# Routed attention and a PReLU feed-forward: a half's attention in one clump instead of three steps

## The chip, the cores and the metric

The kernel runs on one core of one Trainium2 chip. Its time is the device time of one execution in microseconds (us). The engines are TensorE (PE, matmuls; its weight loads are listed as PEld), VectorE (DVE), ScalarE (ACT), GpSimd (POOL) and SyncE (SP, whose queue issues the DMAs). Each engine works through its own list of instructions in order and waits on semaphores for the others. Matmul operands come from SBUF, results go to PSUM, eight banks of 128 partitions x 512 FP32 values.

## The reference

There are 4 batches, 8 heads, 768 positions, head dimension 64 and 16 clusters. A query attends only to keys of its own cluster. The result, with the heads side by side, goes through a feed-forward layer (FFN) from 512 to 2048 and back to 512, with a learned slope for negative values. Everything is FP32 but the weights of the FFN, which arrive as 64-bit floats.

```python
q_assign = np.argmax(np.einsum('bhsd,hcd->bhsc', q_n, c_n), axis=-1)
k_assign = np.argmax(np.einsum('bhsd,hcd->bhsc', k_n, c_n), axis=-1)
mask = q_assign[:, :, :, None] == k_assign[:, :, None, :]
scores = np.where(mask, scale * np.matmul(q, k.transpose(0, 1, 3, 2)), -1e9)
attn = softmax(scores)                      # over the keys
x = np.matmul(attn, v)                      # (B,H,S,D) -> (B*S, H*D)
h = x @ w_in
out = (np.maximum(h, 0.0) + alpha * np.minimum(h, 0.0)) @ w_out
```

## The kernel before

**Units.** Heads are taken in pairs (`pairs`, 16 of them: 4 batches x 4). The 768 queries of a pair are two halves of 384 (`HS`), the keys six chunks of 128 (`NJ`). For a batch, first half 0 of all four pairs is done, then half 1 of all four; when the four are complete, 384 rows of the FFN's input (`xT`) are. The list `steps` holds 96 steps: batch, half, pair, and s = 0, 1, 2, each with two key chunks (`GROUP`). `UB` = 12 steps belong to one half of a batch.

**A step of attention.** `score` makes the transposed scores of two chunks for both heads (line 444: two heads in the upper and lower 64 rows of PE, side by side, into `ps_s`, two tiles of two PSUM banks) and takes their exponentials (line 460, ACT) into E tiles. `weigh` multiplies V by the E tiles of the step before (line 546, two heads in the left and right 64 columns of PE, into the one bank of `ps_v`). `mask` multiplies E by "cluster of the query equals cluster of the key" (line 469, DVE, one instruction for each chunk and head). In batch 0 the mask comes instead from an extra matmul (line 454). `add_up` sums the E tiles over the chunks (lines 482 and 487, DVE) and, after the last chunk, transposes and reduces the sum (lines 492, 495); `total` finishes the denominators with a matmul against a constant (`fold`, line 505) and `invert` takes their reciprocals and spreads them (lines 516 to 523, DVE). `normalise` multiplies the weighted values by them into `xT` (line 569, DVE). An FP32 matmul stands as two instructions in the profile, so counts of matmuls there are double.

**FFN.** `ffn_pieces` cuts the FFN of 384 rows into 28 pieces: 8 `hidden` pieces, then 6 `final` ones, then again 8 and 6. A hidden piece is four matmuls of 384 columns (line 590, into `ps_f`, two banks), then on ACT the positive part (line 597, tile gT) and the negated negative part (line 598, tile `neg`, two buffers). The slope is applied by DVE (line 582, `slopes`); it is emitted in the next hidden piece's call, and after every fourth hidden piece at once. A final piece is four matmuls of 512 columns (line 609) with gT as weights; every second one ends a PSUM bank, which ACT copies (line 615) or DVE adds to the copy (line 617), and after the last one SP sends the rows out (line 620).

**Preparation.** For a pair with first step u, `load` is called at step u-7. From batch 1 on `prep_blocks` transposes q and k on DVE at u-4, `prep_sims` makes the similarities to the centroids on PE at u-3 (line 345), and one slot later `prep_argmax` takes five DVE instructions (lines 353 to 367) to the first-ranked cluster; `prep_clusters` spreads it by PE at u-2 (line 390) and, after an ACT copy, `prep_keys` builds the keys' table; `prep_queries` transposes the queries' table at u-1, for each half. All these use the one bank of `ps_m` (`misc`).

**Order.** The program is written in the order in which each engine is to work. The main loop does, for step u: the scores of u, the weighting of u-1, the masks of u, the normalising of u-1, the sums of u, and then three slots in which FFN pieces of the half batch that is already complete, preparation and (in batch 0 and early) the conversion of FFN weights are placed. `tick` moves a slot counter on, and `later` puts a piece some slots off. FFN pieces are handed out evenly over the 12 steps; two of them (`KEEP`) are left over to the next block.

Of the kernel before, what the change touches and what calls it, by code (L numbers as in the profile page):

```python
# [21 lines left out]
def kernel(  # L22
# [36 lines left out]
    fsp = fast.enter_context(tc.tile_pool(name="fsp", bufs=4))  # L59
    aqp = fast.enter_context(tc.tile_pool(name="aqp", bufs=2))  # L60
    asg = fast.enter_context(tc.tile_pool(name="asg", bufs=1))
    raws = fast.enter_context(tc.tile_pool(name="raws", bufs=5))
    cvt = fast.enter_context(tc.tile_pool(name="cvt", bufs=3))
    epool = fast.enter_context(tc.tile_pool(name="epool", bufs=2 * GROUP))
    accp = fast.enter_context(tc.tile_pool(name="accp", bufs=2))
    rdp = fast.enter_context(tc.tile_pool(name="rdp", bufs=1))
    xpool = fast.enter_context(tc.tile_pool(name="xpool", bufs=2))
# [154 lines left out]

    CW = 512

    def convert(src, dst):
        raw = raws.tile([P, CW, 2], U32, name="raw")
        nc.sync.dma_start(out=raw.rearrange("p n w -> p (n w)"), in_=src)
        lo, hi = raw[:, :, 0], raw[:, :, 1]
        power = cvt.tile([P, CW], U32, name="power")

        def split():
            nc.vector.tensor_scalar(out=power, in0=hi, scalar1=0x7FF00000, scalar2=None,
                                    op0=ALU.bitwise_and)
            nc.vector.tensor_scalar(out=dst.bitcast(U32), in0=hi, scalar1=0x000FFFFF,
                                    scalar2=None, op0=ALU.bitwise_and)

        def scale():
            nc.scalar.activation(out=power, in_=power, func=AF.Relu,
                                 bias=low_exp[:, 0:1], scale=8.0)
            nc.scalar.activation(out=dst, in_=dst.bitcast(U32), func=AF.Identity,  # L240
                                 bias=1.0, scale=2.0 ** -20)

        def join():
            nc.vector.scalar_tensor_tensor(
                out=power, in0=hi, scalar=0x80000000, in1=power,
                op0=ALU.bitwise_and, op1=ALU.bitwise_or)
            nc.vector.scalar_tensor_tensor(  # L247
                out=dst, in0=lo, scalar=2.0 ** -52, in1=dst,
                op0=ALU.mult, op1=ALU.add)
            nc.gpsimd.tensor_tensor(out=dst, in0=dst, in1=power.bitcast(FP32),  # L250
                                    op=ALU.mult)
        return [split, scale, join]
# [177 lines left out]
             for hp in range(NCH) for s in range(SB)]  # L430
    NS = len(steps)
    UB = NCH * SB
    Es, accs, pos, rds, xTs = {}, {}, {}, {}, {}

    def score(u):
        n, half, s = steps[u]
        qkT = qkTs[n]
        chunks = range(s * GROUP, (s + 1) * GROUP)
        pss = [ps_s.tile([P, 2, 512], FP32, name="sps") for c in chunks]
        early_mask = n < NCH  # L440
        for c, ps in zip(chunks, pss):
            for h in range(2):
                r = h * D
                nc.tensor.matmul(  # L444
                    out=ps[:, h, 0:HS],
                    lhsT=qkT[r:r + D, S + c * P:S + (c + 1) * P],
                    rhs=qkT[r:r + D, half * HS:(half + 1) * HS], start=True,
                    stop=not early_mask)
        if early_mask:
            for c, ps in zip(chunks, pss):  # L450
                g, i = divmod(NJ + c, GT)
                r = slice(g * Q, (g + 1) * Q)
                for h in range(2):
                    nc.tensor.matmul(  # L454
                        out=ps[:, h, 0:HS], lhsT=members[n][r, h, i * P:(i + 1) * P],
                        rhs=aqs[n, half][r, 0, :], start=False, stop=True)
        Es[u] = []
        for ps in pss:
            E = epool.tile([P, 2, HS], FP32, name="E")
            nc.scalar.activation(out=E, in_=ps[:, :, 0:HS], func=AF.Exp, scale=SCALE)  # L460
            Es[u].append(E)

    def mask(u):
        n, half, s = steps[u]
        if n < NCH:
            return
        for c, E in zip(range(s * GROUP, (s + 1) * GROUP), Es[u]):
            for h in range(2):
                nc.vector.scalar_tensor_tensor(  # L469
                    out=E[:, h, :], in0=aqs[n, half][:, h, :],  # L470
                    scalar=keys[n][:, NJ + c, h:h + 1],
                    in1=E[:, h, :], op0=ALU.is_equal, op1=ALU.mult)

    def add_up(u):

        n, half, s = steps[u]
        if u < UB:
            return
        E = Es[u]
        if s == 0:  # L480
            acc = accp.tile([P, 2, HS], FP32, name="acc")
            nc.vector.tensor_tensor(out=acc, in0=E[0], in1=E[1], op=ALU.add)
            accs[n, half] = acc
            E = E[2:]
        acc = accs[n, half]
        for e in E:
            nc.vector.tensor_tensor(out=acc, in0=acc, in1=e, op=ALU.add)  # L487
        if s == SB - 1:


            accT = accp.tile([P, 2 * NX, Q], FP32, name="acc")
            nc.vector.transpose(out=accT.rearrange("p x i -> p (x i)"),  # L492
                                in_=acc.rearrange("p h q -> p (h q)"))
            part = rdp.tile([P, 2 * NX], FP32, name="part")
            nc.vector.tensor_reduce(out=part, in_=accT, axis=AX.X, op=ALU.add)  # L495
            parts[n, half] = part

    parts, totals = {}, {}

    def total(u):  # L500

        n, half, s = steps[u]
        if s == SB - 1 and u >= UB:
            ps = misc()
            nc.tensor.matmul(out=ps[:, 0:2 * NX], lhsT=fold, rhs=parts.pop((n, half)),  # L505
                             start=True, stop=True)
            totals[n, half] = ps

    def invert(u):

        n, half, s = steps[u]
        if (n, half) not in totals:
            return
        ps = totals.pop((n, half))
# [10 lines left out]
                in_=inv[r, h * NX:(h + 1) * NX, None].broadcast_to((D, NX, Q)))  # L525
        rds[n, half] = rd

    def weigh(u):


        n, half, s = steps[u]
        E = Es.pop(u)
        if s == 0:
            pos[n, half] = ps_v.tile([P, 512], FP32, name="vps")
        po = pos[n, half]
        if u < UB:
            for i, e in enumerate(E):
                for h in range(2):
                    r = h * D
                    nc.tensor.matmul(out=first_den[r:r + D, 0:HS], lhsT=ones,  # L540
                                     rhs=e[:, h, :], start=(s == 0 and i == 0),
                                     stop=(s == SB - 1 and i == GROUP - 1))
        for c, e in zip(range(s * GROUP, (s + 1) * GROUP), E):
            for h in range(2):
                r = h * D
                nc.tensor.matmul(out=po[r:r + D, 0:HS], lhsT=vts[n][:, h, c, :],  # L546
                                 rhs=e[:, h, :], start=(c == 0), stop=(c == NJ - 1))
        if s == SB - 1 and u < UB:


            denT = asg.tile([P, NX, Q], FP32, name="simT")
# [8 lines left out]
            nc.vector.transpose(out=rd, in_=inv[:, 0:NX, None].broadcast_to((P, NX, Q)))  # L560
            rds[n, half] = rd

    def normalise(u):
        n, half, s = steps[u]
        b, hp = pairs[n]
        if s == SB - 1:
            if (b, half) not in xTs:
                xTs[b, half] = xpool.tile([P, NCH, HS], FP32, name="xT")
            nc.vector.tensor_tensor(out=xTs[b, half][:, hp, :],
                                    in0=pos.pop((n, half))[:, 0:HS],  # L570
                                    in1=rds.pop((n, half)), op=ALU.mult)


    def ffn_pieces(b, half):
        xT = xTs[b, half]
# [27 lines left out]
        def final(i, f0, on, off):  # L603
            convert_up_to((f0 // FQ + 1) * (NCH + FQ))
            if on:
                pss[i] = ps_f.tile([P, 512], FP32, name="fps")
            ps = pss[i]
            for f in range(f0, f0 + FQ):
                nc.tensor.matmul(out=ps[:, 0:DM], lhsT=gs[f][:, i * P:(i + 1) * P],  # L609
# [25 lines left out]
    for u, (n, half, s) in enumerate(steps):  # L635
        start_of.setdefault((n, half), u)

    SLOTS, FIRST = 5, 2
    AHEAD = 4
    prep_at, load_at = {}, {}  # L640
    for (n, half), u in start_of.items():
        def at(step, slot, piece):
# [14 lines left out]

    KEEP = 2
    ffn = deque()
    for u in range(-AHEAD, NS + 1):  # L660
        for n in load_at.get(u, []):
            if n > 1:
                load(n)
        tick()
        if 0 <= u < NS:
            score(u)
        tick()
        if u > 0:
            invert(u - 1)
            weigh(u - 1)  # L670
        if 0 <= u < NS:
            mask(u)
        if u > 0:
            normalise(u - 1)
        if 0 <= u < NS:
            add_up(u)
        if u > 0 and u % UB == 0:
            early.clear()
            n, half, _ = steps[u - 1]
            ffn.extend(ffn_pieces(pairs[n][0], half))  # L680
            whole = len(ffn) - KEEP
        if u == NS:
            break
        take = (max(len(ffn) - KEEP - whole * (UB - 1 - u % UB) // UB, 0) if ffn else 0)
        converting = 0 if u < 0 else 1 + (u % 4 == 3) if u < UB else 1 + u % 2
        for i in range(SLOTS - FIRST):
            tick()
            for _ in range(take * (i + 1) // 3 - take * i // 3):
                ffn.popleft()()
            if (u, i) == (1 - AHEAD, 0):  # L690
                cT, alpha_neg = prepare_constants()
            for piece in prep_at.pop((u, FIRST + i), []):
                piece()
            if i < converting:
                convert_next()
        if 0 <= u < NS:
            total(u)
    while due:
        tick()
    good = const.tile([P, 2], FP32, name="good")  # L700
# [169 lines left out]
```

## Time and profile before

| What | Value |
|---|---|
| time, median of 3 runs | 1048.01 us (1046.67 to 1048.5) |
| the profiled execution | 1049.33 us, of which the span of instructions 1047.5 us |
| mean granted TensorE clock | 0.993 |
| PE, DVE, ACT, POOL busy | 98%, 64%, 33%, 5% of the span |
| DMA | 42.72 MB, mean 41 GB/s |

The page gives the busy time of each engine, the chain of work that ended last, and groups of instructions by line. The trace behind it can be asked for the order of time in a stretch (start, length, engine, line, operation, number of instructions run together, and in brackets how long the engine had been idle and what ended that), for the chain step by step (start, length, what), and for busy time and granted clock in chosen windows. Names before `<-` are what is written, names behind it what is read. A busy PE is not PE at its peak: matmuls overlap, and the distance between the starts of two of them is what counts.

### The profile page before, as it was taken

How to read it: one execution, taken by the hardware profiler on the slowest of the kernel's cores; microseconds unless marked ns; L12 is line 12 of the kernel's file. 1: busy time of each engine (PE TensorE's matmuls, PEld its weight loads, DVE VectorE, ACT ScalarE, POOL GpSimd, SP SyncE). 2: the span in 40 equal slices, each digit the busy share in tenths (PEclk: the TensorE clock that was granted, in tenths of full speed). 3: DMA queues.
4: the chain of work that ended last, by engine and by line, in shares of the span. 5: the costliest groups of instructions: out<-in, count | busy, mean ns of one | idle time of the engine just before them, and what ended most of it. 6: DMA issues, size and time to landing. Idle time of an engine off the chain costs nothing.

```text
span 1047.5 us, 10241 instructions
## 1 busy us (share of the span) xinstructions
PE 1027.5 (98%) x3827; PEld 483.5 (46%) x3827; DVE 675.6 (64%) x1155; ACT 345.6 (33%) x628; POOL 55.8 (5%) x71
## 2 busy tenths in 40 slices
PE   8999999799999999999999999999999999999997
PEld 4444444344454444445444444544445454544553
DVE  4896879758676564868766574876777575562111
ACT  5664443433242323314323132422323132220220
POOL 1332312200000000000000000000000000000000
PEclk9999999899999999999999999999999999999999
DMA  9542663130000230042000230033000000000000
GB/s 217 172 136 81 132 121 76 30 76 1 0 1 21 41 45 16 1 80 42 1 1 11 51 46 16 1 65 56 1 1 0 21 11 1 0 11 20 1 1 33
DMA packets 120936, 42.72 MB, mean 41 GB/s; under 512 B 113696, under 2 KB 113712, under 8 KB 120880
## 3 DMA queue, kind: packets, MB, share of 16 engines
q1 hardware_dynamic: 120704, 41.95, 18.7%
q8 instruction: 32, 0.52, 0.2%
q14 instruction: 24, 0.20, 0.1%
q10 hardware_dynamic: 176, 0.04, 0.0%
HBM read 35.69 MB, written 6.29 MB: 40 GB/s over the span
## 4 chain that ended last, share of the span: by engine, by line
PE 93%; DVE 3%; ACT 1%; DMA 1%; issue 1%; SPq 1%; POOL 0%; DVEq 0%; POOLq 0%; ACTq 0%
PE fps L609 32%; PE fps L590 32%; PE sps L444 13%; PE vps L546 12%; PE sps L454 1%; PE mps L345 1%; PE fps L540 1%; DMA raw<-in_moe_w_in_dram 1%; SPq L114 1%; ACT E L460 0%; DVE gT L582 0%; DMA qk<-in_k_dram 0%; PE mps L505 0%; ACT qk L320 0%; DVE acc L487 0%
## 5 line engine op out<-in xcount | busy, mean ns | idle before, releaser
L609 PE MATMUL fps<-w_out_sb,gT 128*128 128x512 f32 x768 | 347.0, 604 | 6.2 <-POOL w_out_sb L250 6.0
L590 PE MATMUL fps<-xT,w_in_sb 128*128 128x384 f32 x1024 | 345.6, 491 | 0.0
L590 PEld LDWEIGHTS fps<-xT,w_in_sb 128*128 128x128 f32 x1024 | 190.6, 190 | 151.0 <-ACT E L460 18.5
L469 DVE SCALAR_TENSOR_TENSOR E<-aq,key,E 128x384 f32<-128x384 bf16 x288 | 158.9, 613 | 142.5 <-ACT E L460 141.6
L609 PEld LDWEIGHTS fps<-w_out_sb,gT 128*128 128x128 f32 x768 | 142.5, 191 | 194.2 <-issue 176.8
L460 ACT ACTIVATE E<-sps 128x768 f32<-128x768 f32 x192 | 145.4, 808 | 153.8 <-PE sps L444 64.1
L597 ACT ACTIVATE gT<-fps 128x384 f32<-128x384 f32 x128 | 62.7, 490 | 339.2 <-PE fps L590 339.2
L444 PE MATMUL sps<-qkT 64*128 64x384 f32 x768 | 151.2, 512 | 0.0
L546 PE MATMUL vps<-E,vt 128*64 128x384 f32 x768 | 145.0, 499 | 0.0
L582 DVE SCALAR_TENSOR_TENSOR gT<-neg,alpha_neg,gT 128x384 f32<-128x384 f32 x128 | 82.7, 663 | 83.8 <-ACT neg L598 83.7
L487 DVE TENSOR_TENSOR acc<-acc,E 128x768 f32<-128x768 f32 x112 | 107.0, 955 | 19.4 <-ACT E L460 17.0
L444 PEld LDWEIGHTS sps<-qkT 64*128 64x128 f32 x768 | 66.6, 187 | 65.9 <-issue 34.4
L546 PEld LDWEIGHTS vps<-E,vt 128*64 128x64 f32 x768 | 47.8, 136 | 82.3 <-issue 78.6
L617 DVE TENSOR_TENSOR y<-y,fps 128x512 f32<-128x512 f32 x30 | 20.5, 683 | 80.9 <-PE fps L609 80.9
L615 ACT COPY y<-fps 128x512 f32<-128x512 f32 x24 | 14.0, 585 | 158.3 <-PE fps L609 158.3
L598 ACT ACTIVATE neg<-fps 128x384 f32<-128x384 f32 x128 | 62.2, 486 | 5.1 <-DVE gT L582 4.6
L523 DVE STREAM_TRANSPOSE rd<-inv 64x384 f32<-64x384 f32 x56 | 32.1, 573 | 0.4
L250 POOL TENSOR_TENSOR w_in_sb<-w_in_sb,power 128x512 f32<-128x512 f32 x16 | 26.4, 1654 | 85.7 <-DVE w_in_sb L247 85.7
L250 POOL TENSOR_TENSOR w_out_sb<-w_out_sb,power 128x512 f32<-128x512 f32 x16 | 24.8, 1550 | 64.6 <-DVE w_out_sb L247 64.6
L492 DVE STREAM_TRANSPOSE acc<-acc 128x768 f32<-128x768 f32 x28 | 27.4, 978 | 1.0
L495 DVE TENSOR_REDUCE part<-acc 128x24 f32<-128x768 f32 x28 | 26.7, 953 | 1.0
L320 ACT ACTIVATE qk<-qk 128x768 f32<-128x768 f32 x32 | 26.7, 845 | 0.0
(90 smaller groups left out, 434.8 us busy)
## 6 DMA issues: line engine op xcount, KB each, us to landing
raw<-in_moe_w_in_dram SPq DMA_DIRECT2D x16, 512.0 KB, 4.2
raw<-in_moe_w_out_dram SPq DMA_DIRECT2D x16, 512.0 KB, 3.6
vt<-in_v_dram SPq DMA_DIRECT2D x16, 384.0 KB, 4.6
out_dram<-y SPq DMA_DIRECT2D x24, 256.0 KB, 2.1
qk<-in_q_dram SPq DMA_DIRECT2D x48, 96.0 KB, 3.4
qk<-in_k_dram SPq DMA_DIRECT2D x48, 96.0 KB, 3.7
qk<-in_q_dram SPq DMA_DIRECT2D x8, 192.0 KB, 4.9
qk<-in_k_dram SPq DMA_DIRECT2D x8, 192.0 KB, 4.6
```

What stands on the lines that cost most here:

```text
L250: nc.gpsimd.tensor_tensor(out=dst, in0=dst, in1=power.bitcast(FP32), op=ALU.mult)
L444: nc.tensor.matmul(out=ps[:, h, 0:HS], lhsT=qkT[r:r + D, S + c * P:S + (c + 1) * P], rhs=qkT[r:r + D, half * HS:(half + 1) * HS], start=Tr ...
L460: nc.scalar.activation(out=E, in_=ps[:, :, 0:HS], func=AF.Exp, scale=SCALE)
L469: nc.vector.scalar_tensor_tensor(out=E[:, h, :], in0=aqs[n, half][:, h, :], scalar=keys[n][:, NJ + c, h:h + 1], in1=E[:, h, :], op0=ALU.is ...
L487: nc.vector.tensor_tensor(out=acc, in0=acc, in1=e, op=ALU.add)
L523: nc.vector.transpose(out=rd[r, :], in_=inv[r, h * NX:(h + 1) * NX, None].broadcast_to((D, NX, Q)))
L546: nc.tensor.matmul(out=po[r:r + D, 0:HS], lhsT=vts[n][:, h, c, :], rhs=e[:, h, :], start=(c == 0), stop=(c == NJ - 1))
L582: nc.vector.scalar_tensor_tensor(out=gs[f], in0=neg, scalar=alpha_neg[:, f:f + 1], in1=gs[f], op0=ALU.mult, op1=ALU.add)
L590: nc.tensor.matmul(out=ps[:, 0:HS], lhsT=w_in_sb[:, c, f * P:(f + 1) * P], rhs=xT[:, c, :], start=(c == 0), stop=(c == NCH - 1))
L597: nc.scalar.activation(out=gs[f], in_=ps[:, 0:HS], func=AF.Relu)
L598: nc.scalar.activation(out=neg, in_=ps[:, 0:HS], func=AF.Relu, scale=-1.0)
L609: nc.tensor.matmul(out=ps[:, 0:DM], lhsT=gs[f][:, i * P:(i + 1) * P], rhs=w_out_sb[:, f, :], start=on and f == f0, stop=off and f == f0 + ...
```

## The change

Batch 0 keeps its loop. From step `TOGETHER` = 24 on, the attention of a half stands together once every three steps: scores of chunks 0 to 2, weighting of all six chunks of the half that came ahead, masks and sums of the three, then scores, masks and sums of chunks 3 to 5. The rest of the three steps holds FFN pieces, twelve slots for each half. Since `ps_s` has room for two chunks only, chunk 2 of the first three and chunk 3 of the second three (`alone`) go to the two banks of `ps_f`, with one exponential for each head. E tiles are no longer a rotating pool but nine fixed tiles: four of their own and, once the FFN weights are converted (`more_room`), the five raw tiles of the conversion. `total` comes at the first slot of the third step and `invert` at its second, so ahead of the next clump. No FFN piece is kept over to the next block except one at the last, and a final piece that has begun a bank is followed by the one that ends it before the next clump. The steps and slots of loads and preparation are as before (those of slots 2 and 3 in a clump's step now stand behind the whole clump).

```diff
-    raws = fast.enter_context(tc.tile_pool(name="raws", bufs=5))
+    raws = fast.enter_context(tc.tile_pool(name="raws", bufs=1))
-    epool = fast.enter_context(tc.tile_pool(name="epool", bufs=2 * GROUP))
+    epool = fast.enter_context(tc.tile_pool(name="epool", bufs=1))
...
+    raw_tiles = [raws.tile([P, CW, 2], U32, name=f"raw{i}") for i in range(5)]
...
+    waiting = []
+    e_tiles = [epool.tile([P, 2, HS], FP32, name=f"E{i}") for i in range(2 * GROUP)]
+
+    def more_room():
+        for raw in raw_tiles:
+            e_tiles.insert(0, raw.rearrange("p n w -> p (n w)").bitcast(FP32)[
+                :, 0:2 * HS].rearrange("p (h q) -> p h q", h=2))
+
+    def score(n, half, chunks, alone=None):
...
+        pss = [[ps_f.tile([P, 512], FP32, name="fps") for h in range(2)] if c == alone else
+               ps_s.tile([P, 2, 512], FP32, name="sps") for c in chunks]
...
+        for c, ps in zip(chunks, pss):
+            E = e_tiles[0]
+            e_tiles.append(e_tiles.pop(0))
+            if c == alone:
+                for h in range(2):
+                    nc.scalar.activation(out=E[:, h, :], in_=ps[h][:, 0:HS], func=AF.Exp,
+                                         scale=SCALE)
+            else:
+                nc.scalar.activation(out=E, in_=ps[:, :, 0:HS], func=AF.Exp, scale=SCALE)
+            waiting.append((n, half, c, E))
...
+    for u in range(TOGETHER, NS + 1):
+        for n in load_at.get(u, []):
+            load(n)
+        if u < NS:
+            n, half, s = steps[u]
+        if s == 0 or u == NS:
+            prior = steps[u - 1][:2]
+            assert not unfinished[0]
+            tick()
+            if u < NS:
+                score(n, half, range(0, NJ // 2), alone=NJ // 2 - 1)
+            tick()
+            invert(*prior)
+            weigh(GROUP if u == TOGETHER else NJ)
+            if u < NS:
+                mask(NJ // 2)
+            normalise(*prior)
+            if u % UB == 0:
+                feed_block(u)
+                whole = len(ffn) - (NS - u <= UB)
+            if u == NS:
+                break
+            add_up(NJ // 2)
+            tick()
+            score(n, half, range(NJ // 2, NJ), alone=NJ // 2)
+            mask(NJ // 2)
+            add_up(NJ // 2)
+            slots = range(3, SLOTS)
+        else:
+            slots = range(SLOTS)
+        for i in slots:
+            tick()
+            if s == 0:
+                prepare(u, FIRST + i - 3)
+            if (s, i) == (SB - 1, 0):
+                total(n, half)
+            at_slot = (u % UB) // SB * FREE + (s * SLOTS + i - 3)
+            left = UB // SB * FREE - 1 - at_slot
+            pieces = len(ffn) - (NS - u <= UB) - whole * left // (UB // SB * FREE)
+            feed(max(pieces, 0))
+            if (s, i) == (SB - 1, SLOTS - 1) and unfinished[0]:
+                feed(1)
+            if s > 0:
+                prepare(u, i)
+            if (s, i) == (SB - 1, 1):
+                invert(n, half)
```

## The prediction

> **What bounds the kernel now.** I read the page's busy times and the chain of work first, then the chain step by step, then the order of time in one half of batch 2, then the granted clock around TensorE's three long gaps.
>
> ```profile
> PE 1027.5 (98%) x3827; PEld 483.5 (46%) x3827; DVE 675.6 (64%) x1155; ACT 345.6 (33%) x628; POOL 55.8 (5%) x71
> PE 93%; DVE 3%; ACT 1%; DMA 1%; issue 1%; SPq 1%; POOL 0%; DVEq 0%; POOLq 0%; ACTq 0%
> ```
>
> TensorE (PE) is never without work, so only what lies between matmuls can be won. The chain shows it:
>
> ```profile
> 806.30 1.49 PE sps L444 x8
> 807.79 1.44 PE vps L546 x8
> 809.23 7.06 PE fps L609 x16
> 816.29 1.49 PE sps L444 x8
> ...
> 826.29 0.14 PE mps L505 x2
> ...
> 950.43 8.76 PE fps L609 x16
> 959.19 20.64 PE fps L590 x64
> 979.83 20.60 PE fps L609 x48
> ```
>
> The last block, without attention, gives the pace: 20.64/64 = 0.3225 us for a 384-column matmul, 20.60/48 = 0.429 for a 512-column one. Scores and weightings run two heads at once, so 8 are four slots, 1.29. In a step scores take 1.49 (0.20 too much), weighting 1.44 (0.15), 16 final matmuls 7.06 against 6.87 (0.20): **0.55 us a step is lost at changes of kind**. The fold matmul adds 0.14.
>
> The order of time shows VectorE (DVE), which works its queue in order:
>
> ```profile
> 509.43 1.56 PE L444 MATMUL sps<-qkT 64*128 64x384 f32 x8
> 510.40 1.51 ACT L460 ACTIVATE E<-sps 128x768 f32<-128x768 f32 x2 [0.27 <-PE sps L444]
> 511.24 2.21 DVE L469 SCALAR_TENSOR_TENSOR E<-aq,key,E 128x384 f32<-128x384 bf16 x4 [5.56 <-ACT E L460]
> 513.36 1.94 DVE L487 TENSOR_TENSOR acc<-acc,E 128x768 f32<-128x768 f32 x2
> 515.34 0.98 DVE L492 STREAM_TRANSPOSE acc<-acc 128x768 f32<-128x768 f32 x1
> 516.35 0.95 DVE L495 TENSOR_REDUCE part<-acc 128x24 f32<-128x768 f32 x1
> 517.22 0.57 DVE L422 STREAM_TRANSPOSE aq<-every 128x384 bf16<-128x384 bf16 x1
> ```
>
> Masks follow each other by 0.53, adds by 0.98, transpose and reduction by 1.01 and 0.87. Exp starts 0.97 after scores, masks 1.81 after. The argmax that follows the centroid matmuls (L345) has five DVE instructions, 527.05 to 529.78.
>
> The clock, window by window (half-rate spans lasted 3.41 and 10.24 us, one and three times the same stretch, so I cut time in its steps; columns: stretch, length, PE busy and so on; PEclk is third from last):
>
> ```profile
> 43.14:46.55 3.41, 2.07 (x16) 1.06 (x12) 3.38 (x7) 3.41 (x7) 1.71 (x1) 1.00 0.25 36
> 46.55:49.96 3.41, 3.10 (x18) 1.60 (x20) 3.35 (x6) 1.76 (x4) 1.78 (x2) 1.00 0.75 269
> 947.67:951.08 3.41, 1.60 (x10) 0.67 (x7) 2.51 (x10) 0.00 (x0) 0.00 (x0) 1.00 0.20 77
> 951.08:954.50 3.42, 3.42 (x5) 1.33 (x5) 0.00 (x0) 0.00 (x0) 0.00 (x0) 0.50 0.00 0
> ```
>
> A stretch with 1.34 of 3.41 us idle left the clock at 1.00; one with 1.81 idle was followed by 3.42 us at half clock, where 16 final matmuls took 8.76 instead of 7.06: **1.7 us for one such stretch**.
>
> **The change part by part.** Batches 1 to 3 have 24 halves of one head pair, each three steps before, one clump after. T is time since a clump's first score.
>
> *Changes of kind.* Before, per half: 3 x 0.55 + 0.14 = 1.79. After: scores 0.20, weighting 0.15, scores again, feed-forward (FFN) 0.20, fold. Weighting-to-scores and scores-to-FFN do not occur in this trace; the second scores cost between 0.10 and 0.25 by the rows above, I take 0.20, the scores' own row. The fold moves in among FFN matmuls: two 24-column matmuls whose weight loads (190 ns) nothing covers; between 0.20 and 0.40, I take 0.33, from the 0.14 plus what FFN-to-scores costs anyway. After: 1.08. Gain 0.71 x 24 = 17.0. The centroid matmuls (11 times) now stand behind the scores rather than amid FFN, one change less, 0.20 each: -2.2. The cluster matmuls (L390, 11 times) move from behind the weighting into FFN: about +0.1 each, +1.1. **Sum -18.1**, by the bounds -24 to -15.
>
> *No cost.* PE, DVE and DMA issue the same instructions; only the two lone chunks of a half have their exp in two (0.387 + 0.49 against 0.81), with ACT 33% busy. Loads are issued at the same steps, three steps (some 30 us) ahead of their use against 5 us to land, and SP's queue holds only these and the outputs. Both ps_f banks are free at the clump: the last FFN piece's two evictions end at T=0.98, chunk 2's scores start at 1.40. Exp of chunks 0 to 2 ends at 3.26, the second scores need it at 6.15. Nine E tiles suffice for six waiting chunks and three new.
>
> *The DVE burst.* This is the cost. PE: scores of three chunks 6 x 0.3225 + 0.20 = 2.13; weighting of six, 12 x 0.3225 + 0.15 = 4.02, ends 6.15; scores 2.13, so **FFN starts at 8.28** (before it started 2.93 after the scores). DVE: six masks from 1.81 to 5.0; normalise (0.47) waits for weighting, 6.27 to 6.74; two adds (0.98 + 0.88) to 8.60; six masks to 11.78; three adds to 14.74; transpose to 15.76; reduction to **16.63**. Behind it in the queue stand the slopes (L582, pitch 0.53, done after 0.61) of hidden pieces and, in 11 halves, the argmax: 0.61 + 0.59 + 0.59 + 0.39 to its last instruction, 0.55 more to its result. A hidden piece takes 8 x 0.3225 = 2.58, a final piece 8 x 0.429 = 3.43, FFN's first 0.10 more. Seven pieces go into each clump, so clumps 0, 2, 4, 6 of a batch begin with hidden pieces, and 1, 3, 5, 7 with the last of eight hidden, the slope of the seventh still owing. Centroid matmuls (0.78) stand ahead of FFN in clumps 0, 1, 2 and (not in the last batch) 7; the cluster matmuls, which need the argmax, come only three pieces later, where before they came a step later.
>
> - Clumps 4, 6: nothing late. The third hidden's neg tile comes free at 17.3, its bank at 17.8, the fifth hidden wants it at 18.7.
> - Clumps 0, 2: FFN from 9.07, three hidden end at 8.28 + 0.78 + 0.10 + 7.74 = 16.91. The argmax is there at 16.63 + 2.18 + 0.55 + 0.06 (release) = 19.43. **PE waits 2.5**. Five such clumps (clump 0 of batch 1 is covered by two final pieces held back): 12.6.
> - Clumps 3, 5 (and 7 of batch 3): hidden to 10.97, final to 14.40, two weights of the next final to 16.12; the third needs the seventh slope, 16.63 + 0.61 + 0.06, and its weight load 0.19: 17.50. PE waits 1.38, seven times: 9.7.
> - Clumps 1, 7: 0.78 later at the same place, wait 0.60; then clusters at 19.22 against the argmax behind two slopes, 17.69 + 2.18 + 0.55 + 0.06 = 20.48, wait 1.27. Four times 1.87: 7.5. Clump 1 of batch 1, with eight pieces behind it: hidden, hidden, final end at 17.76, argmax behind one slope at 20.0: 2.2.
>
> **Sum +32.0**; each 0.1 us on the burst's end is worth 1.7. From both sides: the burst cannot start before its first exp, and 0.4 us either way is what I allow for releases and pitches, +-7.
>
> *Clock.* Idle of 2.2 to 2.5 us, six times: where it falls in one 3.41-us stretch, or over 1.6 of it does, half clock follows. With stretches placed at random that is about five in six (threshold between the 1.34 and the 1.81 seen): 5 x 1.7 = **+8.5**, between 0 and two stretches each, 20. Waits of 1.4 us I leave at full clock, the row of 1.34 being nearest. The trace itself has 203.6 to 213.8 at half clock, untouched by the change.
>
> The Trainium skill's page "TensorE: Matmul & The Clock Gate", section "HAM oscillation — how this bites in real kernels", has a rule against idle gaps over about 3.4 us; read strictly, none of these waits would cost clock and the sum would be 8.5 lower. The row of 947.67 disagrees: there a gap of 1.81 us sufficed, so I go by the row.
>
> *End.* The inversion now precedes the last weighting, so the flag matmul waits for normalise and four small instructions only: 1.2 instead of 1.8 us, which by the rows leaves the clock up: -0.6 - 1.7 = **-2.3**.
>
> Sum: -18.1 + 32.0 + 8.5 - 2.3 = +20.1. The profiled execution took 1049.33 (span 1047.5 and 1.83 around it): 1069.4. The median, 1048.01, lies 1.3 below that execution, so I say 1068.
>
> **Rivals.**
> 1. *The clock stays up* at all waits. For: the 1.34 row. Against: the 1.81 row. 1059.6.
> 2. *The clock falls further*: also at the waits of 1.4 and 1.9 us (eleven, about half of them), or for two stretches where a wait straddles them; the three stretches from 203.6, one of them 85% busy, speak for it. 10 us more, 1078.
> 3. *Faster: the burst is covered.* If DVE reaches the slopes and the argmax 0.85 us sooner than 16.63, the waits shrink to 18 and almost no clock falls, and gain and loss balance; 2 us sooner leaves some 3 us of waits, and the time is near 1031. For: DVE is only 64% busy, and 1.3 us of the burst is its wait for weighting. Against: its pitches are in every step of this trace.
> 4. *The change does not do what it says*: the two unseen changes of kind cost as much as three steps did. Then 17.0 is lost and it is 1085. Every change seen costs 0.15 to 0.20, against it.
>
> **How the numbers follow.** Forecast (1060 to 1077) 0.45; rival 1 (1050 to 1060) 0.20; rivals 2 and 4 (over 1077) 0.16; rival 3 (under 1046) 0.15; balance by chance 0.04. 0.2% (2.1 us) is about what this kernel's measurement can tell from no change. The range, 1047 to 1085, leaves out the faster case and the far end; the forecast's own range is 1060 to 1077. Faster 0.15, same 0.04, slower 0.81.
>
> **What would show it.** Right: PE idle before the cluster matmuls, ended by the argmax's last reduction, some 2.5 us; PE idle before final matmuls, ended by the slopes, 1.4 us, in the later half of each batch; short stretches at half clock after the former; changes of kind down to some 0.75 us a half; the gap before the flag matmul near 1.2. Wrong: PE as closed as before in batches 1 to 3, or DVE through its burst well before T=16.

## The result and the profile after

| | before | after |
|---|---|---|
| median of the runs | 1047.95 us (1046.67 to 1048.5, 4 runs) | 1062.31 us (1059.04 to 1064.19, 4 runs) |
| profiled execution | 1049.33 | 1059.04 |
| PE, DVE, ACT busy | 98%, 64%, 33% | 95%, 64%, 33% |

The changed kernel is slower: its time is 1.0135 of the time before, 95% interval 1.0109 to 1.0162. 1068 was forecast. The page, engines and chain:

```profile
PE 1008.8 (95%) x3827; PEld 488.5 (46%) x3827; DVE 679.3 (64%) x1155; ACT 346.4 (33%) x676; POOL 55.9 (5%) x71
PE 71%; DVE 24%; issue 1%; ACT 1%; DMA 1%; SPq 0%; POOL 0%; DVEq 0%; POOLq 0%; ACTq 0%
```

TensorE is busy 18.7 us less for the same matmuls (fewer changes of kind, and 6.83 us at half clock instead of 13.65), and yet the span grew: DVE, with the same work as before, holds 24% of the chain instead of 3%. Which waits these are, the view of PE's waits says (in all, times, longest):

```profile
PE mps L393 <- DVE first L370: 18.5, 10, 2.3
PE fps L631 <- DVE gT L603: 8.2, 12, 1.0
PE fps L611 <- DVE y L639: 2.8, 2, 2.4
PE mps L796 <- DVE good L793: 1.2, 1, 1.2
```

Before, the same view of 300 to 930 us lists no wait of PE at all. L393 are the cluster matmuls, L370 the last reduction of the argmax; L603 are the slopes. One clump (clump 2 of batch 1, T = 0 at 280.81) in order of time, PE and DVE:

```profile
280.81 1.56 PE L461 MATMUL sps<-qkT 64*128 64x384 f32 x8
...
282.62 2.20 DVE L494 SCALAR_TENSOR_TENSOR raw<-aq,key,raw 128x384 f32<-128x384 bf16 x4 [11.25 <-ACT raw L482]
...
287.08 0.56 DVE L588 TENSOR_TENSOR xT<-vps,rd 128x384 f32<-128x384 f32 x1 [1.21 <-PE vps L567]
287.56 0.95 DVE L505 TENSOR_TENSOR acc<-raw,raw 128x768 f32<-128x768 f32 x1
...
289.41 3.26 DVE L494 SCALAR_TENSOR_TENSOR E<-aq,key,E 128x384 f32<-128x384 bf16 x6
289.88 8.01 PE L611 MATMUL fps<-xT,w_in_sb 128*128 128x384 f32 x24
292.59 2.93 DVE L510 TENSOR_TENSOR acc<-acc,E 128x768 f32<-128x768 f32 x3
...
296.57 0.95 DVE L518 TENSOR_REDUCE part<-acc 128x24 f32<-128x768 f32 x1
297.44 0.57 DVE L356 STREAM_TRANSPOSE simT<-mps 128x384 f32<-128x384 f32 x1
...
299.62 0.55 DVE L370 TENSOR_REDUCE first<-top 128x24 bf16<-128x384 bf16 x1
300.23 0.26 PE L393 MATMUL mps<-first,spread 128*128 128x24 bf16 x4 [2.34 <-DVE first L370]
```

DVE's burst runs from 282.62 (T = 1.81) to the argmax's first instruction at 297.44 (T = 16.63, as worked out in the prediction). PE has done its three hidden pieces at 297.89 and stands 2.34 us until the argmax is there. In the clock's windows (columns as in the prediction), this wait and the one before the flag matmul:

```profile
296.40:299.81 3.41, 1.49 (x5) 0.57 (x3) 3.24 (x7) 0.49 (x1) 0.00 (x0) 1.00 0.00 0
299.81:303.22 3.41, 2.99 (x15) 1.93 (x15) 2.46 (x6) 0.63 (x3) 0.00 (x0) 1.00 0.02 5
...
968.82:972.23 3.41, 3.12 (x11) 1.90 (x12) 0.36 (x2) 0.12 (x1) 0.00 (x0) 1.00 0.00 0
```

Here 1.92 us of a stretch were idle and the clock stayed; no half-rate stretch shows in this execution between 211 us and the end of the matmuls. The three other runs were slower by 3 to 5 us, at mean clocks of 0.992, 0.989 and 0.992 against 0.995; they left no trace, so where their clock fell is not known.

### The profile page after: what moved, and what is told of

Read it like the earlier page. It is cut to its first block, busy times and chain, and to the rows that moved or that the text cites. A ratio compares the mean times of both kernels' runs of the same rounds, so it can differ in the third digit from the quotient of the medians.

```text
span 1057.3 us, 10220 instructions
## 1 busy us (share of the span) xinstructions
PE 1008.8 (95%) x3827; PEld 488.5 (46%) x3827; DVE 679.3 (64%) x1155; ACT 346.4 (33%) x676; POOL 55.9 (5%) x71
## 3 DMA queue, kind: packets, MB, share of 16 engines
q1 hardware_dynamic: 120704, 41.95, 18.5%
## 4 chain that ended last, share of the span: by engine, by line
PE 71%; DVE 24%; issue 1%; ACT 1%; DMA 1%; SPq 0%; POOL 0%; DVEq 0%; POOLq 0%; ACTq 0%
PE fps L631 24%; PE fps L611 24%; PE vps L567 11%; PE sps L461 7%; DVE acc L510 7%; DVE raw L494 3%; DVE E L494 2%; PE fps L461 2%; DVE acc L515 2%; DVE part L518 2%; DVE acc L505 1%; DVE gT L603 1%; PE sps L471 1%; PE fps L562 1%; DVE xT L588 1%
## 5 line engine op out<-in xcount | busy, mean ns | idle before, releaser
L603 DVE SCALAR_TENSOR_TENSOR gT<-neg,alpha_neg,gT 128x384 f32<-128x384 f32 x128 | 83.1, 666 | 97.9 <-ACT neg L619 97.5
L494 DVE SCALAR_TENSOR_TENSOR raw<-aq,key,raw 128x384 f32<-128x384 bf16 x160 | 87.3, 611 | 44.3 <-ACT raw L482 44.3
L461 PE MATMUL sps<-qkT 64*128 64x384 f32 x576 | 110.5, 502 | 0.0
L482 ACT ACTIVATE E<-sps 128x768 f32<-128x768 f32 x88 | 67.2, 813 | 82.2 <-PE sps L471 44.9
L494 DVE SCALAR_TENSOR_TENSOR E<-aq,key,E 128x384 f32<-128x384 bf16 x128 | 70.3, 611 | 20.5 <-ACT E L482 20.5
L567 PE MATMUL vps<-E,vt 128*64 128x384 f32 x448 | 81.4, 491 | 0.0
L639 DVE TENSOR_TENSOR y<-y,fps 128x512 f32<-128x512 f32 x30 | 20.5, 684 | 91.9 <-PE fps L631 91.9
L510 DVE TENSOR_TENSOR acc<-acc,E 128x768 f32<-128x768 f32 x64 | 61.2, 957 | 19.1 <-ACT E L482 16.9
L482 ACT ACTIVATE raw<-sps 128x768 f32<-128x768 f32 x56 | 42.9, 814 | 70.1 <-PE sps L461 70.1
L567 PE MATMUL vps<-raw,vt 128*64 128x384 f32 x320 | 56.5, 491 | 0.0
L510 DVE TENSOR_TENSOR acc<-acc,raw 128x768 f32<-128x768 f32 x48 | 45.8, 955 | 1.1
L461 PE MATMUL fps<-qkT 64*128 64x384 f32 x192 | 41.4, 508 | 0.0
```

Source lines behind the costliest of these rows:

```text
L461: nc.tensor.matmul(out=bank(ps, h), lhsT=qkT[r:r + D, S + c * P:S + (c + 1) * P], rhs=qkT[r:r + D, half * HS:(half + 1) * HS], start=True, ...
L494: nc.vector.scalar_tensor_tensor(out=E[:, h, :], in0=aqs[n, half][:, h, :], scalar=keys[n][:, NJ + c, h:h + 1], in1=E[:, h, :], op0=ALU.is ...
L603: nc.vector.scalar_tensor_tensor(out=gs[f], in0=neg, scalar=alpha_neg[:, f:f + 1], in1=gs[f], op0=ALU.mult, op1=ALU.add)
```

## The experiments

The theory: the gain at changes of kind is there, but a half's masks and sums, now in one piece of DVE's queue, make the argmax and the slopes late, and PE, which works in order, waits; long waits now and then cost clock. The rivals: PE is held by something else (banks, ACT), or the clump itself costs PE time. Ratios are to the kernel before on the same chip, whose medians there lay between 1045.72 and 1048.3.

### The suspected cause taken away: no masks in clumps

```diff
-            if n < NCH:
+            if n < NCH or m == NJ // 2:
                 continue
```

> The masks of the clumps are left out (twelve VectorE instructions for each half, so queries of batches 1 to 3 attend to all keys). It takes away the suspected cause: the burst ends some 3.2 us sooner (not 6.4, since the second sums then wait for the exponentials). Theory: all waits but the one of clump 0 of batch 1 go, some 30 us, and what is left is the gain from fewer changes of kind: 1028 to 1031, profile and median alike. Rival (changes of kind gain nothing, or clumps cost TensorE time by themselves): over 1040.

Measured: **1024.3** (1024.13 to 1024.74), 0.978 of before (0.976 to 0.980). The page's chain and, in PE's waits, all that is longer than 0.2 us and lies behind batch 0:

```profile
PE 95%; DVE 3%; ACT 1%; issue 1%; POOL 0%; DVEq 0%; POOLq 0%
```

```profile
PE mps L796 <- DVE good L793: 1.2, 1, 1.2
```

Of the waits behind batch 0 only the one at the end is left (L796, before the flag matmul); that of clump 0 of batch 1 is gone too. Between the profiled executions, 1059.04 and 1024.74, lie 34.3 us: the price of the waits (PE's view lists 29.5 us of idle for them; what makes the rest was not taken apart). From before's 1049.33 to 1024.74 are 24.6. How much of it is changes of kind, sixteen halves of a head pair tell, in which neither execution is at half clock: from the first scores of half 1 of batch 1 to those of half 1 of batch 3 the kernel before takes 490.87 us (335.49 to 826.36), this run 477.09 (334.70 to 811.79). That is 0.86 a half, 20.7 in 24. The end has about 2.3; the remaining 1.6 lie in batch 0, where the half-rate stretch falls on other work. The clump costs PE nothing by itself.

### One mover moved: the cluster matmuls two slots later

```diff
-                at(u - 2, FIRST, lambda n=n: prep_clusters(n))
+                at(u - 2, FIRST + 2 if u - 2 >= TOGETHER else FIRST,
+                   lambda n=n: prep_clusters(n))
```

> From the first clumps on, the cluster matmuls (L390 before, L393 after) are placed two slots later; nothing else is changed. Theory (the VectorE burst makes the argmax late, and TensorE, working in order, stands at the cluster matmuls): the 18.5 us of idle before them go. What is behind the argmax in VectorE's queue, the slopes, now holds TensorE in its place: about 1.0 us in each of the five clumps 0 and 2 at the fifth hidden piece's bank, 1.2 us in clump 1 of batch 1. So some 12.5 us off the profiled 1059: about 1047 in the profile, and a median no more than 2 us above it, since no wait is left that could pull the clock down. Rival (TensorE is held by its banks or by ScalarE, and the argmax is only the last to come): the idle moves to another line in the same size, 1059 to 1062. Rival (changes of kind became dearer): no change of time.

Measured: **1055.72** (1055.44 to 1056.91), a ratio of 1.0082 (1.0062 to 1.0102). The wait before L393 is gone, but only 3 us came of it in the profiled execution (1055.99). PE's waits, and the place in order of time:

```profile
PE mps L527 <- ACT every L397: 9.5, 11, 1.6
PE fps L631 <- DVE gT L603: 9.0, 13, 1.0
...
PE fps L611 <- ACT neg L619: 3.2, 4, 0.8
```

```profile
301.12 0.25 PE L393 MATMUL mps<-first,spread 128*128 128x24 bf16 x4
301.55 0.49 ACT L619 ACTIVATE neg<-fps 128x384 f32<-128x384 f32 x1 [2.32 <-DVE gT L603]
301.94 0.48 ACT L618 ACTIVATE gT<-fps 128x384 f32<-128x384 f32 x1
302.31 0.50 ACT L619 ACTIVATE neg<-fps 128x384 f32<-128x384 f32 x1
302.68 0.26 ACT L397 CAST every<-mps 128x96 bf16<-128x96 f32 x1
302.99 0.40 PE L527 MATMUL mps<-part,fold 128*128 128x24 f32 x2 [1.62 <-ACT every L397]
```

The waits at the hidden pieces' bank came as expected (four of 0.8). What I had not seen: two slots later the cluster matmuls stand directly ahead of the fold, and both use the one bank of `ps_m`. ACT's copy out of it stands behind three evictions that are themselves late because of the slopes. So I expected too much, by the size of a wait that took the place of the one removed.

### The same with the fold and the inversion two slots later

```diff
-            if (s, i) == (SB - 1, 0):
+            if (s, i) == (SB - 1, 2):
                 total(n, half)
...
-            if (s, i) == (SB - 1, 1):
+            if (s, i) == (SB - 1, 3):
                 invert(n, half)
```

> As the run with the cluster matmuls two slots later, and the fold two slots and the inversion two slots later, so that a feed-forward piece stands between cluster matmuls and fold. In the run without this TensorE waited 9.5 us at the fold for the cluster matmuls' bank, which ScalarE had yet to copy. Theory: that wait goes, 1055.7 - 9.5, so 1045 to 1047; left are the slopes' waits, some 12 us with the fifth hidden piece's. Rival (the fold waits for something else than the bank): 1053 to 1056.

Measured: **1046.37** (1045.29 to 1047.91), 1.0002 of before (0.9991 to 1.0013): 9.4 less than without the second step, the wait at the fold is gone, and it was the bank.

### The slope of the last hidden piece ahead of a clump emitted at once

```diff
-            if f % FQ == FQ - 1:
+            if f % FQ == FQ - 1 or f % (2 * FQ) == 2 * FQ - 2:
                 slopes()
```

> The slope of the hidden piece that stands last before a clump is emitted in that piece's own call, so ahead of the burst instead of behind it. Theory: the waits of final matmuls for gT shrink. In the seven clumps without centroid matmuls only the eighth slope is left behind the burst, 0.5 us instead of 1.4 each, 6 us; in the four with them the argmax moves up by one slope, 0.5 each, 2 us. So 8 us off: 1051 in the profile, a median near 1054; the waits of the cluster matmuls in clumps 0 and 2 stay at 2.3 us. Rival (the final matmuls wait for PSUM or the copies): 1059 to 1062, the waits as they were.

Measured: **1055.08** (1054.86 to 1056.43), a ratio of 1.0078 (1.0058 to 1.0098). The waits for gT went from 8.2 to 1.0 us; those of the cluster matmuls stayed (19.0). The profiled execution, 1054.94, shows three half-rate stretches after batch 0, two of them in these windows, each behind a wait at the cluster matmuls:

```profile
258.45:261.86 3.41, 0.86 (x4) 0.05 (x3) 3.27 (x8) 0.49 (x1) 0.00 (x0) 1.00 0.00 0
261.86:265.28 3.42, 3.42 (x8) 1.56 (x9) 0.93 (x3) 0.24 (x1) 0.00 (x0) 0.50 0.02 5
480.31:483.73 3.42, 1.07 (x7) 0.39 (x6) 3.28 (x8) 0.49 (x2) 0.00 (x0) 1.00 0.00 0
483.73:487.15 3.42, 3.42 (x7) 1.89 (x6) 1.11 (x2) 0.62 (x2) 0.00 (x0) 0.50 0.00 0
```

Three times 1.7 are 5.1: without them it would stand at 1049.8, a little under the 1051 expected.

### The gaps filled, to part the clock from the waiting

```diff
         ps = misc()
+        for _ in range((3 if n % NCH % 2 else 1) if n > NCH else 0):
+            nc.tensor.matmul(out=ps[:, 0:HS], lhsT=ident, rhs=qkTs[n][:, 0:HS],
+                             start=True, stop=True)
         for g in range(NG):
```

> Ahead of the cluster matmuls TensorE gets matmuls whose result is thrown away, three of 384 columns (1.94 us) in clumps 0 and 2, one (0.65 us) in 1 and 7, into the bank that the cluster matmuls then write. They stand where TensorE waits anyway, so the time without clock effects stays at 1059 within 1 us, while no idle gap is over 1.3 us. Theory (the runs' spread of 1059 to 1064 and their clocks of 0.995 to 0.989 come from gaps of 2.3 us that fall into one window of the clock or not): every run at 1059 to 1060, clock 0.994 to 0.995. Rival (the spread is of another origin): median 1062 and the same spread.

Measured: **1060.64**, four runs within 1060.54 to 1060.65 and one at 1062.19, clocks 0.994 to 0.996. The waits before the cluster matmuls are down to 3.5 us in all, the waits for gT unchanged at 8.2, and no half-rate stretch lies behind 212 us. The runs of the changed kernel spread over 5.2 us, and their clock falls as their time grows; with the gaps filled four of five lie within 0.1. That fits the theory but does not prove it: there are few runs, the run with the slope emitted early keeps gaps of 2.3 us and spread over 1.6 only, and the kernel before, without any of these waits, spread over 4.5 us on the same chip.

The profiled 1060.65 lies 1.6 over the changed kernel's 1059.04. The fill costs this where PE did not wait at the cluster matmuls, in clump 0 of batch 1:

```profile
231.84 2.10 PE L393 MATMUL mps<-qkT,ident 128*128 128x384 f32 x6
```

From the second scores of clump 0 to the first of clump 1 pass 30.08 us (214.52 to 244.60) instead of 28.51 (214.67 to 243.18). So the expectation that it stands only where TensorE waits anyway was wrong in this one clump. Where PE did wait, the fill cost nothing: the sixteen halves take 499.64 us, in the changed kernel 499.72. The longer half-rate stretch of this execution in batch 0 (10.24 us against 6.83) is not the reason: behind it the two kernels are level.

### The burst made longer

```diff
             parts[n, half] = part
+            spent = rdp.tile([P, 2 * NX], FP32, name="spent")
+            nc.vector.tensor_reduce(out=spent, in_=accT, axis=AX.X, op=ALU.add)
```

> The changed kernel with the last reduction of each burst done twice, the second time into a tile that nobody reads: 0.98 us more VectorE work at the end of each burst. Theory: seventeen waits grow by 0.98 each, and two sorts of clump that had 0.9 us to spare now just wait: 17 us, so 1076 in the profile if the clock stays; six waits of 3.3 us fill a window of the clock, so that half clock follows most of them, up to 10 us more: 1076 to 1088, clock 0.985 to 0.99. Rival (TensorE is not held by the burst's end): under 1066.

Measured: **1091.23** (1089.73 to 1094.63), clocks 0.976 to 0.981, a little over the range expected. PE's waits, and two pairs of windows:

```profile
PE mps L393 <- DVE first L370: 23.7, 10, 3.2
PE fps L633 <- DVE gT L605: 17.6, 12, 1.9
```

```profile
489.69:493.10 3.41, 0.71 (x3) 0.09 (x1) 3.27 (x7) 0.49 (x1) 0.00 (x0) 1.00 0.00 0
493.10:496.52 3.42, 2.92 (x9) 1.71 (x10) 2.12 (x4) 0.62 (x2) 0.00 (x0) 0.50 0.00 0
...
329.27:332.68 3.41, 1.54 (x5) 0.47 (x4) 3.38 (x5) 0.00 (x0) 0.00 (x0) 1.00 0.00 0
332.68:336.10 3.42, 3.42 (x5) 1.34 (x5) 0.28 (x2) 0.00 (x0) 0.00 (x0) 0.50 0.00 0
```

Seventeen waits grew by 0.86 to 0.87 each, the distance between two reductions that don't depend on each other rather than 0.98, 14.6 us in all. The other half of the 31 us between the profiled executions is clock: nine windows, 30.7 us, at half rate behind 214 us. At 1.7 each they are worth 15.3, more than expected, since the waits of 1.87 at the final matmuls now trigger it as well (the second pair).

### Two DVE steps exchanged

In every clump of the changed kernel behind which PE waits, but the very first, the chain goes through the weighting, here in clump 2 of batch 1:

```profile
283.01 4.04 PE vps L567 x24
287.06 0.02 issue
287.08 0.56 DVE xT L588
287.64 0.88 DVE acc L505
```

So there DVE's 1.21 us of waiting before normalise is not slack. The sums of the first three chunks need only the masks; they can go ahead of it.

```diff
-            normalise(*prior)
+            if u < NS:
+                add_up(NJ // 2)
+            normalise(*prior)
...
-            add_up(NJ // 2)
             tick()
             score(n, half, range(NJ // 2, NJ), alone=NJ // 2)
```

> The changed kernel with two VectorE steps of a clump exchanged: the sums of the first three chunks come before the normalising of the half ahead, which has to wait for TensorE's weighting. No instruction is added or left out. Theory: VectorE no longer stands 1.2 us for the weighting in mid burst; its second masks are then held by the exponentials, so the burst ends some 0.9 us sooner, and with it each of the eighteen waits: 16 us less of them, 1042 to 1044 in the profile and the median, since no gap of over 1.9 us is left to pull the clock down. Rival (that wait of VectorE is slack; what is behind it is held by ScalarE): 1057 to 1062.

Measured: **1043.15** (1042.72 to 1043.18), 0.9957 of before (0.9943 to 0.9971), and 16 us less than the profiled execution of the changed kernel. In order of time, DVE in the same clump, whose first score starts at 279.68:

```profile
284.66 0.95 DVE L505 TENSOR_TENSOR acc<-raw,raw 128x768 f32<-128x768 f32 x1
285.65 0.96 DVE L510 TENSOR_TENSOR acc<-acc,E 128x768 f32<-128x768 f32 x1
286.53 0.55 DVE L588 TENSOR_TENSOR xT<-vps,rd 128x384 f32<-128x384 f32 x1
287.30 3.29 DVE L494 SCALAR_TENSOR_TENSOR E<-aq,key,E 128x384 f32<-128x384 bf16 x6 [0.23 <-ACT E L479]
...
295.36 0.57 DVE L356 STREAM_TRANSPOSE simT<-mps 128x384 f32<-128x384 f32 x1
```

The burst ends at T = 15.68 instead of 16.63. The waits of the cluster matmuls fell from 18.5 to 11.0, those for gT from 8.2 to 0.2.

### Everything moved behind the burst

Eight hidden or six final pieces follow a clump, so no slope is owing when one begins; the argmax comes one slot later, behind the first slope; cluster matmuls and fold are moved so that a piece lies between them.

```diff
-        later(1, lambda: prep_argmax(n, ps))
+        later(2 if n > NCH else 1, lambda: prep_argmax(n, ps))
...
-                at(u - 2, FIRST, lambda n=n: prep_clusters(n))
+                at(u - 2, FIRST + 1 + u // SB % 2 if u - 2 >= TOGETHER else FIRST,
+                   lambda n=n: prep_clusters(n))
...
-            at_slot = (u % UB) // SB * FREE + (s * SLOTS + i - 3)
-            left = UB // SB * FREE - 1 - at_slot
-            pieces = len(ffn) - (NS - u <= UB) - whole * left // (UB // SB * FREE)
-            feed(max(pieces, 0))
+            slot = s * SLOTS + i - 3
+            if slot == 0:
+                share = len(ffn) - (20 if u % UB < 6 else 6) if (u // SB) % 2 == 0 else 6
+            feed(-(-share * (slot + 1) // FREE) + (share * slot // -FREE))
```

Besides, `total` and `invert` stand one slot later each.

> All that the burst held up is moved behind it, and the clump itself is left as it is: a clump is followed by eight hidden or six final pieces instead of seven of either (no slope is owing when a clump begins), the argmax is emitted one slot later (behind the first slope), the cluster matmuls one or two slots later, and the fold one slot later, so that a piece stands between the cluster matmuls and it and the bank they share is free. Theory: all waits but the one of clump 0 of batch 1 (2 to 3 us) and some 0.4 us in clumps 0 and 2 go; 1024 as without masks, plus 3 to 5: 1027 to 1030, clock 0.994, faster than before by 1.8%. Rival (a clump's VectorE work only fits when masks are left out; what is moved finds a new wait): 1040 or more.

Measured: **1026.92** (1026.76 to 1027.21), 0.9812 of before (0.9791 to 0.9833). This version, with its masks, beats both kernels, and by the most. PE's waits behind batch 0:

```profile
PE fps L611 <- DVE y L639: 1.4, 1, 1.4
...
PE mps L797 <- DVE good L794: 1.2, 1, 1.2
```

The sixteen halves take 477.09 us, to the digit what they took without masks, against 499.72 in the changed kernel. So there the whole loss came from the order of the work behind the burst, and not from the amount of DVE's work.

Two additions to it brought nothing. Without pieces kept back from batch 0:

```diff
-            whole = len(ffn) - KEEP
-        take = (max(len(ffn) - KEEP - whole * (UB - 1 - u % UB) // UB, 0) if ffn else 0)
+            whole = len(ffn)
+        take = (max(len(ffn) - whole * (UB - 1 - u % UB) // UB, 0) if ffn else 0)
```

> As the run with even shares, and no FFN pieces of batch 0 are kept back for the first clump. Theory: the first hidden piece no longer waits for an addition of y that stands behind the burst (2 to 3 us); 1025 to 1027. Rival (the kept pieces then wait ahead of the clump for the same addition): as the run with even shares.

Measured: **1032.15** (1031.76 to 1034.37). Neither theory had this: with KEEP = 0 the same 28 pieces are handed out earlier in batch 0, before the weights that they need are converted; the wait for y is gone, but PE waits five times for POOL's conversion instead of twice, and the half-rate stretch there lasts 17.07 us instead of 10.24. With the exchange of the two DVE steps:

> The run with even shares, with the same exchange. Theory: there only the wait of clump 0 of batch 1 is left (1.4 us), which shrinks by 0.9; 1026 against 1026.9, at the edge of what can be told. Rival (the later normalising makes the first hidden piece of a block wait): 1028 or more.

Measured: **1027.23** (1026.82 to 1028.47), as without. The one wait left was 2.1 us in this execution, not shorter.

## Why the prediction was right, and where it was off

**Direction and cause: right.** The forecast was slower, by waits of PE for a burst in DVE's queue, at the cluster matmuls and at the slopes. Both stand in PE's waits; removing the burst's masks removes all of them, lengthening it lengthens them, and ending it 0.95 sooner ends 16 us of them.

**The DVE burst: right to the digit.** End worked out at T = 16.63, measured 16.63 in the clump shown. Clumps 0, 2: wait 2.5 forecast, 2.34 of idle measured, five times. Clumps 3, 5: 1.38 forecast with the weight load of 0.19, 1.01 of idle, seven times. Clumps 1, 7: 0.60 + 1.27 forecast, 0.2 + 1.20. Clump 1 of batch 1: 2.2 against 2.01. Clumps 4, 6: none, as said. **The step that failed here**: clump 0 of batch 1 "is covered by two final pieces held back". It waited 2.8, for the additions to y (L639) of these very pieces, which stand behind the burst: I counted the pieces as cover and not what they issue on DVE. In sum 32.0 forecast, 34.3 measured.

**Changes of kind: -18.1 forecast, -20.7 measured.** The spells not seen before cost what the rows suggested (six chunks of weighting 4.04 us against 3.87, second scores about 0.20 over their pace). The mis-sized term is the fold among FFN matmuls, taken at 0.33: two matmuls take 0.14 and the next piece another 0.08. That is 2.6 in 24 halves, the whole difference; the terms for the centroid and the cluster matmuls, -2.2 and +1.1, were not measured by themselves.

**Clock: the term that was mis-sized most.** +8.5 was forecast. The profiled execution, 1059.04, shows none of it in these waits, and the median run, 1062.3, lies 3.3 above, at a lower clock. The mechanism is there: in the run with the slope emitted early, 2.35 us of idle in one window were followed by one at half rate. But I drew the line at 1.6 us of idle in a window, between 1.34 and 1.81. Later, windows of 1.92 (here, and with the slope early) did not trigger, one of 1.87 (the longer burst) did; the line lies near 1.8 to 1.9, not sharp by this measure, so a wait of 2.3 has to lie almost whole in one window. These 5 us are most of the 5.8 between 1068.1 and 1062.3; the errors at the changes of kind (-2.6) and at the waits (+2.3) nearly cancel, which is luck. Nor was the stretch at half clock in batch 0 untouched, as I had assumed: it lasted 6.83 us in the profiled execution instead of 10.24, and in the other runs between 6.83 and 17.07. The Trainium skill's page "TensorE: Matmul & The Clock Gate", section "HAM oscillation — how this bites in real kernels", would have idle gaps cost clock from about 3.4 us on. The profile after, taken alone, looks like that; the run with the slope emitted early, with half rate behind waits of 2.35 us, does not, and the measurement decides.

**End: right.** The gap was 1.19 (1.2 forecast) and the clock stayed up behind it.

**Rivals.** Rival 1 (clock up) met the profiled execution, whose 1059.04 falls within its bounds, and not the median. Rival 3 named its turning point, the burst ending 0.85 us sooner; the exchange ended it 0.95 sooner, and the time fell just under that of before. Rival 4 is out. Rival 2 came true only with the longer burst.

## What to carry to other kernels

When work is gathered on one engine to spare it changes of kind, write down the queue of every other engine that follows it: the sum of their work may be the same, but the burst moves everything queued behind it. The wait to look for is at the first instruction of the gathered engine that needs something from behind the burst, and moving that one instruction can hand the wait to the next user of the same bank; move what follows it too. A wait of the off-path engine inside the burst is on the path, and filling it is the cheapest mend: two exchanged steps were worth 16 us here.

## What the runs showed of the hardware

- The clock fell to half for at least 3.41 us after windows of 3.41 us with 1.81 us of idle (before), 1.87 (longer burst), 2.35 and 2.55 (slope early), and stayed up after 1.92 in two executions (changed kernel, slope early); where the windows lie differs between executions. The changed kernel, with gaps near 2 us, spread from 1059 to 1064; with them filled, four of five runs lay between 1060.54 and 1060.65. That such gaps alone make the spread is not shown.
- Each spell of one kind of matmul cost 0.15 to 0.20 us over its own pace in the chains of before and after: scores 1.49 us against 1.29, six chunks of weighting 4.04 against 3.87, 16 final matmuls 7.06 against 6.87. Two 24-column FP32 matmuls amid full ones cost 0.14 and 0.08 more at the next.
- With the extra reduction the waits grew by 0.86 to 0.87 and no more, DVE's pitch between independent reductions, while a dependent sum took 0.98.
